# Folding the per-head maps into k's and q's weights: 64-by-64 tiles of three heads, four side by side, in place of 120 rows by 128 columns, with x's first transposes put ahead of the first modulation sums

## The chip, the cores and the metric

The kernel runs on one core of a Trainium2 chip. The metric is the device time of one execution in microseconds; lower is better. The core has TensorE (PE in the profile, its weight loads PEld), VectorE (DVE), ScalarE (ACT), GpSimd (POOL) and SyncE (SP, which here issues DMA transfers). TensorE writes to PSUM banks, the other compute engines read them. Everything is computed in float32, or in pairs of a rounded "high" part and the rest, the "low" part.

## The reference: what is computed

One transformer block for 2048 tokens of width 640 with 32 heads of 20. A condition vector `c` gives six rows of modulation (shift, scale and gate for each half). Attention is linear: each head's q and k go through a 20-by-20 matrix `w_phi[h]` and a softmax of both signs. A two-layer network with squared ReLU follows.

```
mod = (_silu(c) @ w_mod)                      # sa, ca, ga, sb, cb, gb
h = _layernorm(x) * (1 + ca) + sa
q, k, v = split(h @ wqkv)                     # 32 heads of 20
pq = einsum("bhsd,hdf->bhsf", q, w_phi);  pk = the same of k
phi = concat(softmax(p), softmax(-p))
o = phi_q @ (phi_k^T v) / (phi_q @ sum(phi_k))
x = x + ga * (o @ wo)
h = _layernorm(x) * (1 + cb) + sb
x = x + gb * (relu(h @ w1 + b1)**2 @ w2 + b2)
```

Since `pq` is linear in h, the kernel multiplies q's and k's weights by the heads' matrices once (the fold), and projects h with the folded weights. The change is in this fold.

## The kernel before, in words

**Stages.** The first 34 us load and prepare the weights of k and q, normalise the first 256 tokens and compute the modulation. Then a loop over 16 tiles of 128 tokens projects k, v and q and sums phi_k^T v; a second loop makes the attention's output; a third does the two-layer network. Up to the first projections of q and v, the order of the instructions on all five engines is the order in which the code is written (`manual_schedule`), so the order of the lines 625 to 662 is the order on each engine.

**Loads (lines 208 to 246).** SP issues, in this order: five chunks of k's weights (`load_raw`, lines 213 to 220), x's first 256 tokens, four chunks of q's weights, two chunks `wm` of modulation weights, q's fifth chunk, three more `wm`, x's second 256 tokens, five chunks of v's weights. A chunk of k's or q's weights is 320 KB, one of `wm` and one of x 640 KB. The host has transposed and reordered the weights of k and q: chunk d holds in 120 of 128 rows the features of six heads in each of five groups, and beside them the 128 input features of chunk d as columns. The 40 features of the last two heads lie in an array of their own (100 KB), loaded behind the first chunk.

**Block-diagonal matrix `bd_t` (lines 157 to 162, 248 to 258).** GpSimd makes a mask `own`, which says which of 120 rows belong to which of six heads. VectorE multiplies it with the heads' matrices (`bdc`, loaded by ScalarE's queue) in three operations.

**The fold (`fold`, lines 272 to 292).** For k and for q, and for each of five chunks of 128 input features, TensorE takes the raw weights as the stationary operand, 120 rows by 128 columns, and `bd_t` as the moving one, 120 columns for each of five groups of six heads and 40 for the last. The result, 128 input features by 640, fills two PSUM banks: the first three groups (360 columns) in the first, the rest (280) in the second. Banks come from a pool of four (`pj`, two folds' worth); only the fold of q's chunk 0 uses two banks of `kvp`. In the profile these matmuls are `foldk`, `foldq` and `kvp` of line 282. Each float32 matmul shows as two pairs of LDWEIGHTS and MATMUL, so a fold is 12 pairs.

`split` (lines 287 to 290) then takes each bank: ScalarE copies it to the rounded high part (line 289), VectorE subtracts that from the bank for the low part (the helper `lo`, line 90).

**The order around it (lines 623 to 662).** TensorE warms up with nine matmuls of ones (line 625) while the data come, and does five folds of k and four of q. In between VectorE takes the statistics of x (`stats`, lines 560 and 561, with a few operations on GpSimd, lines 562 to 565), and ScalarE scales x by them (`scale`, line 570). Then come, for chunk 0 of the modulation, `mod_rows2` (line 586: ten small matmuls of 32 columns that spread over four column tiles), `mod_sb` (line 594: ScalarE copies the sums from PSUM, `msb`), the ten transposes of x (`t_in`, line 364), `mod_cols2` (line 599: TensorE transposes `msb`; line 601: VectorE reduces it to shift and scale, `cols_a`), and `out0` (lines 375, 376 and 90: ScalarE applies shift and scale to x and rounds, `hfa` and `hT`; VectorE makes the low part). Chunk 1 of the modulation, q's fifth fold, chunk 2 and then the first projection of k (`k_step`, line 80, `pk`) follow. The split of q's fold 3 is written behind the transposes.

Of the kernel before, what the change touches and what calls it, by code (L numbers as in the profile page):

```python
# [53 lines left out]
def kernel(  # L54
# [19 lines left out]
    nc = tc.nc  # L74
# [14 lines left out]
    def lo(out_lo, full, hi, eng=None):  # L89
        (eng or nc.vector).tensor_tensor(out_lo, full, hi.bitcast(F32), op=ALU.subtract)  # L90
# [4 lines left out]
    def over(ap):  # L95
        return ap[:, :, None].to_broadcast([ap.shape[0], ap.shape[1], DH])
# [28 lines left out]
    def wslot(name, tag="w", pool=None):  # L125
        return tok2(tag, name, W2_AT if name.startswith("w2_") else 0, pool).bitcast(F32R)
# [26 lines left out]
    nc.gpsimd.memset(ones, 1.0)  # L153

    bdc = row("s3", "bdc")
    own = bdc[:120, P : P + 6]
    nc.gpsimd.memset(own, 1.0)
    nc.gpsimd.affine_select(out=own, in_=own, compare_op=ALU.is_ge, fill=0.0, base=0,
                            pattern=[[-DH, 6]], channel_multiplier=1)
    nc.gpsimd.affine_select(out=own, in_=own, compare_op=ALU.is_ge, fill=0.0, base=DH - 1,  # L160
                            pattern=[[DH, 6]], channel_multiplier=-1)
# [43 lines left out]
    nc.gpsimd.tensor_tensor(mask5, mask5, mtmp[:80, :40], op=ALU.add)  # L205


    nc.scalar.dma_start(bdc[:120, :120], bd)
# [12 lines left out]

    def load_x(j):
        XB[j] = tok2(f"x{j % 2}", f"xb{j}")
# [6 lines left out]
    def flat(e):  # L230
        return e.rearrange("p s d -> p (s d)")

    load_raw("k", wk5, wk1)
    load_x(0)
    load_raw("q", wq5, wq1, range(4))
    for d in range(2):
        load_wm(d)
# [7 lines left out]
        RV[d] = both[:, d % 2]  # L245
        nc.sync.dma_start(RV[d], wv[d * P : (d + 1) * P])

    by_head = bdc[:120, :120].rearrange("p (g f) -> p g f", f=DH)
    for a, b in ((0, 3), (3, 5)):
        nc.vector.tensor_tensor(  # L250
            bd_t[:120, 120 * a : 120 * b].rearrange("p (g i f) -> p g i f", i=6, f=DH),
            by_head[:, a:b, None, :].to_broadcast([120, b - a, 6, DH]),
            own[:, None, :, None].to_broadcast([120, b - a, 6, DH]), op=ALU.mult
        )
    nc.vector.tensor_tensor(
        bd_t[:120, 600:].rearrange("p (i f) -> p i f", f=DH),
        by_head[:, 5:6, :].to_broadcast([120, 2, DH]), over(own[:, :2]), op=ALU.mult
    )

    cs = const.tile([P, NC], F32, name="cs")  # L260
# [11 lines left out]
    def fold(nm, d, p=None):  # L272

        w = wslot(f"w{nm}{d}")
        W[nm, d] = w
        p = p or pj(f"fold{nm}{d}")
        for g, (o, n) in enumerate(GR):
            if g < 5:
                r = raw[nm][d // 2][:120, d % 2, g * P : (g + 1) * P]
            else:  # L280
                r = raw[nm][2][:120, 1, d * P : (d + 1) * P]
            nc.tensor.matmul(  # L282
                p[g // 3][:, (g % 3) * 120 : (g % 3) * 120 + n], r, bd_t[:120, g * 120 : g * 120 + n],
                start=True, stop=True,
            )

        def split():
            for h, (a, b) in enumerate(((0, 360), (360, 640))):
                nc.scalar.activation(w[:, 0, a:b], p[h][:, : b - a], AF.Copy)
                lo(w[:, 1, a:b], p[h][:, : b - a], w[:, 0, a:b])  # L290

        return split

# [64 lines left out]
    def by_turn(ap):  # L358
        return ap.rearrange("p (f b) -> p b f", b=NC)

    def t_in(xn, d, p, mixed=False):
        for i in range(2):
            src = by_turn(xn[:, i])[:, d] if mixed else xn[:, i, d * P : (d + 1) * P]
            nc.tensor.transpose(p[:, i * P : (i + 1) * P], src, ident)  # L364
# [207 lines left out]
    def half(b, h):  # L572
        return kvp[b][:, 256 * h : 256 * h + 256]
# [3 lines left out]
    def mod_rows2(*ds):  # L577

        p = tp(f"mrow{ds[0]}")
        for m, d in enumerate(ds):  # L580
            MR[d] = p[:, m * P : m * P + P]
            for k in range(NC):
                for s in range(2):
                    c = 2 * (k % 2) + s
                    a = 256 * k + P * s
                    nc.tensor.matmul(  # L586
                        MR[d][32 * c : 32 * c + 32], cs[:, k : k + 1].to_broadcast([P, 32]), WM[d][:, a : a + P],
                        start=(k < 2 and m == 0), stop=(k >= NC - 2), skip_group_check=True,
                    )

    def mod_sb(*ds):
        for d in ds:
            t = MR[d, "sb"] = row("s1", f"msb{d}")[:, :P]
            nc.scalar.activation(t, MR[d], AF.Identity, bias=plus[:, 0:1])
# [11 lines left out]
    TR = [half(0, 0), half(1, 0), half(1, 1), half(2, 0), half(2, 1)]  # L606
# [19 lines left out]
    for d in range(4):  # L626
        fold("k", d)()
# [16 lines left out]
    split = fold("q", 4)  # L644
# [68 lines left out]
    for t in range(2, NT - 2):  # L713
        j, i = divmod(t, 2)
# [12 lines left out]
        p = proj("v", t, *([(1, 0, lambda: t1(j + 1, 4))] if t == NT - 3 else []))  # L727
# [492 lines left out]
    for j in range(NB):  # L1220
        nxt = j + 1 < NB
        b, c = 2 * j + 5, 2 * j + 6
# [63 lines left out]
        if j == 7:  # L1286
            t2(0, 4)
            p = tp("gbt")[:NC, :P]
# [512 lines left out]
```

## Time and profile before

| | us |
|---|---|
| median of 3 runs (lowest to highest) | 751.52 (750.88 to 751.8) |
| the profiled execution's own time | 751.83 |
| its span, first to last instruction | 750.1 |
| what lies around the span | 1.7 |
| TensorE busy | 744.9 (99%) |
| VectorE, ScalarE, GpSimd busy | 601.4, 457.5, 169.0 |

| stretch, us | TensorE busy | weight loads | VectorE | ScalarE | DMA share, GB/s |
|---|---|---|---|---|---|
| 5.05 to 12.40 (k's folds) | 7.35 | 7.35 | 4.76 | 3.89 | 1.02, 377 |
| 12.40 to 17.86 (q's folds 0 to 3) | 5.46 | 5.41 | 4.06 | 4.13 | 1.04, 410 |
| 17.86 to 23.14 (modulation, fold 4) | 5.28 | 4.40 | 2.94 | 3.56 | 1.02, 408 |
| 23.14 to 34.00 (k's first projection) | 10.86 | 10.49 | 4.88 | 7.71 | 1.04, 388 |

A busy TensorE says little by itself: matmuls overlap, and the length of one (275 ns for one of the fold's) is several times the distance at which they follow each other. The distance is what counts, and it is read from a count of matmuls and the time that they take together. The names on the left of an arrow are written, those on the right read; numbers such as `128x360` are partitions by elements.

### The profile page before, as it was taken

What the parts mean: (1) busy time and instruction counts of PE and PEld (TensorE: products, weight loads), DVE (VectorE), ACT (ScalarE), POOL (GpSimd) and SP (SyncE); (2) the same over time, 40 slices, a digit from 0 to 9 for tenths busy, and PEclk for the clock granted to TensorE, in tenths of its full rate; (3) what the DMA queues carried; (4) which work ended last, traced back from release to release, by engine and by line L of the source; (5) the groups of instructions that cost most, each with busy time, mean ns of one, the idle gap of its engine ahead of it and who ended that gap; (6) DMA issues with size and microseconds to landing.
All of it is one profiled execution on the core that took longest, in us unless ns stands there. A gap on an engine that the chain in (4) does not pass through costs nothing.

```text
span 750.1 us, 15320 instructions
## 1 busy us (share of the span) xinstructions
PE 744.9 (99%) x5854; PEld 728.3 (97%) x5854; DVE 601.4 (80%) x1089; ACT 457.5 (61%) x1065; POOL 169.0 (23%) x355
## 2 busy tenths in 40 slices
PE   9999999999999999999999999999999999999998
PEld 9999999999999998998999999999999999999997
DVE  6598987988998899999665778777777776777766
ACT  5767666667863355557587766475574756647431
POOL 3000101000100237647303040132221313223110
PEclk9999999999999999999999999999999999999999
DMA  9811432343432254663885576797667767667461
GB/s 330 335 36 77 155 93 81 107 140 107 137 101 81 57 189 160 150 148 109 195 236 183 158 212 227 252 343 204 180 198 200 222 183 227 191 172 218 127 184 36
DMA packets 58796, 126.39 MB, mean 168 GB/s; under 512 B 7438, under 2 KB 16403, under 8 KB 58723
## 3 DMA queue, kind: packets, MB, share of 16 engines
q1 hardware_dynamic: 38636, 79.20, 32.2%
q0 software_dynamic: 17504, 40.90, 21.8%
q10 hardware_dynamic: 2583, 5.30, 1.9%
q8 instruction: 46, 0.75, 0.4%
q14 instruction: 27, 0.22, 0.1%
HBM read 100.74 MB, written 29.89 MB: 174 GB/s over the span
## 4 chain that ended last, share of the span: by engine, by line
PE 98%; ACT 1%; DVE 1%; POOL 0%; issue 0%; ACTq 0%; POOLq 0%
PE up L80 25%; PE acc L80 18%; PE pq L80 9%; PE pk L80 9%; PE pv L80 9%; PE pwo L80 9%; PE acc3x L80 5%; PE kvp L457 3%; PE te L954 2%; PE numa L80 1%; PE foldk L282 1%; PE numb L80 1%; PE ta L364 1%; PE foldq L282 1%; PE warm L625 1%; PE mrow L586 1%
## 5 line engine op out<-in xcount | busy, mean ns | idle before, releaser
L80 PE MATMUL up<-h,w 128*128 128x256 f32 x1640 | 204.6, 276 | 0.1
L80 PEld LDWEIGHTS up<-h,w 128*128 128x128 f32 x1640 | 196.5, 188 | 0.7 <-DVE h L90 0.5
L1350 ACT ACTIVATE ft<-up,b_t 128x256 f32<-128x256 f32 x104 | 49.0, 471 | 96.0 <-PE up L80 95.6
L80 PE MATMUL acc<-w,ra 128*128 128x384 f32 x452 | 97.5, 335 | 0.0
L80 PE MATMUL pwo<-wo,ot 128*128 128x384 f32 (+1 forms) x480 | 78.4, 314 | 0.0
L1351 DVE TENSOR_TENSOR ft<-ft 128x256 f32<-128x256 f32 x104 | 43.8, 421 | 43.1 <-ACT ft L1350 41.4
L80 PE MATMUL pq<-wq,hT 128*128 128x384 f32 (+1 forms) x480 | 75.6, 312 | 0.0
L80 PEld LDWEIGHTS acc<-w,ra 128*128 128x128 f32 x452 | 72.7, 188 | 0.8 <-DVE ra L90 0.6
L80 PE MATMUL pk<-wk,hT 128*128 128x384 f32 (+1 forms) x480 | 72.7, 308 | 0.0
L80 PEld LDWEIGHTS pwo<-wo,ot 128*128 128x128 f32 x480 | 69.7, 188 | 2.8 <-issue 2.7
L80 PEld LDWEIGHTS pq<-wq,hT 128*128 128x128 f32 x480 | 71.1, 188 | 0.6 <-issue 0.2
L80 PE MATMUL pv<-wv,hT 128*128 128x384 f32 (+1 forms) x480 | 71.6, 306 | 0.0
L80 PEld LDWEIGHTS pk<-wk,hT 128*128 128x128 f32 x480 | 70.5, 188 | 0.4 <-issue 0.2
L80 PEld LDWEIGHTS pv<-wv,hT 128*128 128x128 f32 x480 | 70.0, 188 | 0.0
L90 DVE TENSOR_TENSOR ra<-ft,ra 128x384 fp32r<-128x384 f32 (+2 forms) x86 | 36.8, 449 | 32.6 <-ACT ra L1374 20.0
L1460 POOL DMA_DIRECT2D ring_a<-td_a x34 | 18.5, 543 | 116.9 <-PE acc L80 103.6
L1374 ACT ACTIVATE ra<-ft 128x384 fp32r<-128x384 f32 x48 | 25.2, 526 | 28.4 <-DVE ft L1351 22.4
L80 PE MATMUL acc3x<-w,ra 128*128 128x256 f32 x231 | 39.5, 278 | 0.0
L80 PEld LDWEIGHTS acc3x<-w,ra 128*128 128x128 f32 x231 | 37.2, 188 | 0.0
L1365 DVE TENSOR_TENSOR ft<-ft 128x128 f32<-128x128 f32 x136 | 33.3, 286 | 1.2
L448 DVE TENSOR_REDUCE sk<-ek 128x64 f32<-128x1280 f32 x16 | 23.7, 1484 | 12.8 <-ACT ek L443 10.8
L341 POOL TENSOR_SCALAR sma<-sma 128x2 f32<-128x2 f32 x6 | 1.8, 298 | 137.2 <-ACT xb L340 137.2
(270 smaller groups left out, 1470.2 us busy)
## 6 DMA issues: line engine op xcount, KB each, us to landing
ring_c<-td_c POOLq DMA_DIRECT2D x34, 384.0 KB, 3.8
ring_a<-td_a POOLq DMA_DIRECT2D x34, 384.0 KB, 3.4
ring_b<-td_b POOLq DMA_DIRECT2D x34, 256.0 KB, 3.6
esp<-eq SPq DMA_DIRECT2D x12, 640.0 KB
el<-esp SPq DMA_DIRECT2D x12, 640.0 KB
rw<-in_w SPq DMA_DIRECT2D x23, 320.0 KB
wm<-in_w_mod SPq DMA_DIRECT2D x20, 320.0 KB
xb<-in_x SPq DMA_DIRECT2D x8, 640.0 KB
```

The lines of the kernel that those rows point to most:

```text
L80: nc.tensor.matmul(o, a, b, start=first and i == 0, stop=last and i == len(terms) - 1, skip_group_check=skip,)
L90: (eng or nc.vector).tensor_tensor(out_lo, full, hi.bitcast(F32), op=ALU.subtract)
L282: nc.tensor.matmul(p[g // 3][:, (g % 3) * 120 : (g % 3) * 120 + n], r, bd_t[:120, g * 120 : g * 120 + n], start=True, stop=True,)
L364: nc.tensor.transpose(p[:, i * P : (i + 1) * P], src, ident)
L448: nc.vector.tensor_reduce(s, heads(flat(e)), axis=AX.X, op=ALU.add)
L457: nc.tensor.matmul(kvp[g // 4][64 * c : 64 * c + 64, a : a + 2 * n].rearrange("p (s n) -> p s n", s=2), v[:, u], e[:, :, o : o + n], start ...
L954: nc.tensor.transpose(p[:124, a : a + P], EU[2 * j + i][:, 2 * g + c, :124], ident)
L1350: nc.scalar.activation(r, p, AF.Relu, bias=b1_t[:, f : f + 1])
L1351: nc.vector.tensor_tensor(r, r, r, op=ALU.mult)
L1365: nc.vector.tensor_tensor(t[:, o], t[:, a], t[:, b], op=op)
L1374: nc.scalar.activation(a[:, 0, :3], t[:, :3], AF.Copy)
L1460: nc.gpsimd.dma_start(RING[j, n, r], TD[n][r].bitcast(F32R))
```

## The change

The fold is cut otherwise. The 32 heads are split in two halves of 16, one on rows 0 to 59 of each chunk and one on rows 64 to 123 (rows 60 to 63 and 124 to 127 are zero); a group is three heads (60 rows) of each half, and there are five groups and one of one head. For each group four matmuls of 64 rows by 64 columns with 60 moving columns (20 in the last group) go to the four quarters of the array: rows 0 and 64, columns 0 and 64. The half by rows selects the PSUM bank, the half by columns its partitions. So a fold has 24 matmuls, 48 pairs, for 6 matmuls and 12 pairs; both banks hold 320 columns and are written until the fold's end. The host lays out the raw weights and the heads' matrices to match, with as many bytes in all for the weights; the last heads' rows come in two transfers of 20 rows. `bd_t` needs one multiply of 360 columns, and the mask one more operation on GpSimd.

In the order, the ten transposes of x come ahead of the first `mod_rows2`, and the split of q's fold 3 directly behind its fold, ahead of `mod_sb`.

```diff
+FOLDS = [(60 * g, 60) for g in range(5)] + [(300, DH)]
...
-                nc.sync.dma_start(raw[nm][2][:40, 1], w1)
+                for a in range(2):
+                    nc.sync.dma_start(raw[nm][2][64 * a : 64 * a + DH, 1], w1[DH * a : DH * a + DH])
...
-        for g, (o, n) in enumerate(GR):
-            if g < 5:
-                r = raw[nm][d // 2][:120, d % 2, g * P : (g + 1) * P]
-            else:
-                r = raw[nm][2][:120, 1, d * P : (d + 1) * P]
-            nc.tensor.matmul(
-                p[g // 3][:, (g % 3) * 120 : (g % 3) * 120 + n], r, bd_t[:120, g * 120 : g * 120 + n],
-                start=True, stop=True,
-            )
+        for g, (o, n) in enumerate(FOLDS):
+            r = raw[nm][d // 2][:, d % 2, g * P : (g + 1) * P] if g < 5 else raw[nm][2][:, 1, d * P : (d + 1) * P]
+            for a in (0, 64):
+                for c in (0, 64):
+                    nc.tensor.matmul(
+                        p[a // 64][c : c + 64, o : o + n], r[a : a + 64, c : c + 64], bd_t[a : a + 64, o : o + n],
+                        start=(g == 0), stop=True, skip_group_check=True,
+                    )
 
         def split():
-            for h, (a, b) in enumerate(((0, 360), (360, 640))):
-                nc.scalar.activation(w[:, 0, a:b], p[h][:, : b - a], AF.Copy)
-                lo(w[:, 1, a:b], p[h][:, : b - a], w[:, 0, a:b])
+            for h, (a, b) in enumerate(((0, HALF), (HALF, D))):
+                nc.scalar.activation(w[:, 0, a:b], p[h][:, :HALF], AF.Copy)
+                lo(w[:, 1, a:b], p[h][:, :HALF], w[:, 0, a:b])
...
-    split = fold("q", 3)
+    fold("q", 3)()
+    for d in range(NC):
+        t_in(XB[0], d, TR[d])
     mod_rows2(0)
     mod_sb(0)
-    for d in range(NC):
-        t_in(XB[0], d, TR[d])
-    split()
     mod_cols2(0)
```

On TensorE, around q's fold 3 and the first modulation sums, before (`foldq` is the fold, `mrow` the sums, `kvp<-ident,xb` the transposes of x, `kvp<-ident,msb` that of the copied sums):

```order
L282 MATMUL foldq_0_357<-bd_t,raw_q_146 128x120 x3
L282 MATMUL foldq_1_358<-bd_t,raw_q_146 128x120 x2
L282 MATMUL foldq_1_358<-bd_t,raw_q_147 128x40
L586 MATMUL mrow_365<-wm_154,cs 32x128 x10
L364 MATMUL kvp_76<-ident,xb_143 128x128 x2
L364 MATMUL kvp_77<-ident,xb_143 128x128 x4
L364 MATMUL kvp_78<-ident,xb_143 128x128 x4
L599 MATMUL kvp_76<-ident,msb_376 128x128
L586 MATMUL mrow_398<-wm_156,cs 32x128 x10
```

The same place with the change, from the last full group of the fold on:

```order
L280 MATMUL foldq_0_502<-bd_t,raw_q_148 64x60 x2
L280 MATMUL foldq_1_503<-bd_t,raw_q_148 64x60 x2
L280 MATMUL foldq_0_502<-bd_t,raw_q_149 64x20 x2
L280 MATMUL foldq_1_503<-bd_t,raw_q_149 64x20 x2
L362 MATMUL kvp_76<-ident,xb_145 128x128 x2
L362 MATMUL kvp_77<-ident,xb_145 128x128 x4
L362 MATMUL kvp_78<-ident,xb_145 128x128 x4
L584 MATMUL mrow_542<-wm_157,cs 32x128 x10
L597 MATMUL kvp_76<-ident,msb_553 128x128
L584 MATMUL mrow_561<-wm_159,cs 32x128 x10
```

The transposes have moved from between the sums and the transposition of `msb` to the front of the sums; the two banks of a fold (`foldq_0`, `foldq_1`) now take turns instead of one after the other.

On ScalarE at the same place, before (`wq<-foldq` are a fold's two copies, `xb` the scaling of x, `hfa` and `hT` the first use of shift and scale):

```order
L570 ACTIVATE xb_143<-xb_143,nba_293,sqa_292 128x640 x2
L289 ACTIVATE wq_343<-foldq_0_344 128x360
L289 ACTIVATE wq_343<-foldq_1_345 128x280
L594 ACTIVATE msb_376<-mrow_365,plus 128x128
L289 ACTIVATE wq_356<-foldq_0_357 128x360
L289 ACTIVATE wq_356<-foldq_1_358 128x280
L375 ACTIVATE hfa_0_394<-kvp_76,cols_a 128x256
```

And with the change:

```order
L568 ACTIVATE xb_145<-xb_145,nba_366,sqa_365 128x640 x2
L287 ACTIVATE wq_470<-foldq_0_471 128x320
L287 ACTIVATE wq_470<-foldq_1_472 128x320
L287 ACTIVATE wq_501<-foldq_0_502 128x320
L287 ACTIVATE wq_501<-foldq_1_503 128x320
L592 ACTIVATE msb_553<-mrow_542,plus 128x128
L373 ACTIVATE hfa_0_557<-kvp_76,cols_a 128x256
```

The copies of q's fold 3 have passed the copy of the first sums. VectorE's order is the same but for the one multiply in place of three; behind this place all engines do what they did, in the same order.

More of the change, by code (lines that the diff above doesn't have):

```diff
@@ L155 @@
     bdc = row("s3", "bdc")
[L156 to L161, printed above, removed]
+    own6 = bdc[:, 120:126]
+    own = own6[:, :3]
+    nc.gpsimd.memset(own6, 1.0)
+    o6 = own6.rearrange("p (a i) -> p a i", a=2)
+    nc.gpsimd.affine_select(out=o6, in_=o6, compare_op=ALU.is_ge, fill=0.0, base=0,
+                            pattern=[[-64, 2], [-DH, 3]], channel_multiplier=1)
+    nc.gpsimd.affine_select(out=o6, in_=o6, compare_op=ALU.is_ge, fill=0.0, base=DH - 1,
+                            pattern=[[64, 2], [DH, 3]], channel_multiplier=-1)
+    nc.gpsimd.tensor_tensor(own, own, own6[:, 3:], op=ALU.add)
     ident = const.tile([P, P], F32, name="ident")
@@ L246 @@
         nc.sync.dma_start(RV[d], wv[d * P : (d + 1) * P])
[L248 to L253, printed above, removed]
-        )
     nc.vector.tensor_tensor(
-        bd_t[:120, 600:].rearrange("p (i f) -> p i f", f=DH),
-        by_head[:, 5:6, :].to_broadcast([120, 2, DH]), over(own[:, :2]), op=ALU.mult
+        bd_t[:, :360].rearrange("p (g i f) -> p g i f", i=3, f=DH),
+        bdc[:, :120].rearrange("p (g f) -> p g f", f=DH)[:, :, None, :].to_broadcast([P, 6, 3, DH]),
+        own[:, None, :, None].to_broadcast([P, 6, 3, DH]), op=ALU.mult
     )
@@ L1762, in by_chunk @@
     def by_chunk(w):
-        t = np.zeros((P, 5, D), w.dtype)
-        t[:120] = w.T[:600].reshape(5, 120, D).transpose(1, 0, 2)
-        return t.reshape(P, 5, NC, P).transpose(2, 0, 1, 3).reshape(NC * P, D), w.T[600:]
+        w = w.T.reshape(2, HALF, D)
+        t = np.zeros((2, 64, 5, D), w.dtype)
+        t[:, :60] = w[:, :300].reshape(2, 5, 60, D).transpose(0, 2, 1, 3)
+        return t.reshape(P, 5, NC, P).transpose(2, 0, 1, 3).reshape(NC * P, D), w[:, 300:].reshape(2 * DH, D)
     wq5, wq1 = by_chunk(A_wqkv[:, :D])
@@ L1779 @@
         "wv": A_wqkv[:, 2 * D :][:, VCOLS],
-        "bd": bd.reshape(120, 120),
+        "bd": bd.reshape(P, 120),
         "c": c.reshape(NC, P).T,
```

8 lines of the change are left out of this document (4 added, 4 removed).

## Prediction

> **What bounds the kernel now.** First the page: who carries the chain that ended last, and at which clock.
>
> ```profile
> PE 98%; ACT 1%; DVE 1%; POOL 0%; issue 0%; ACTq 0%; POOLq 0%
> PEclk9999999999999999999999999999999999999999
> ```
>
> TensorE sets the end nearly everywhere, at full clock. So a microsecond taken off TensorE early in the program is a microsecond off the end, if TensorE does not wait for anything later. The waits of TensorE from 33 us to the end, and the largest of its weight loads', are these:
>
> ```profile
> PE tail L936 <- POOL rn L1160: 0.4, 1, 0.4
> PEld pwo L80 <- issue: 2.7, 7, 0.4
> ```
>
> No engine or transfer makes it wait there for more than a few tenths; what follows the change is carried along. Then the chain in order of time over the first 30 us (start, length, what):
>
> ```profile
> 1.05 4.21 PE warm L625 x18
> 5.26 7.31 PE foldk L282 x60
> 12.57 1.34 PE kvp L282 x12
> 13.91 4.02 PE foldq L282 x36
> 17.93 0.78 PE mrow L586 x20
> 18.71 1.24 PE kvp L364 x10
> 19.95 0.11 PE kvp L599
> 20.06 0.78 PE mrow L586 x20
> 20.84 1.46 PE foldq L282 x12
> 22.30 0.14 PE kvp L599
> 22.44 0.78 PE mrow L586 x20
> ```
>
> The ten folds are TensorE back to back: nine from 5.26 to 17.93, the tenth at 20.84. One fold is 12 pairs of weight load and matmul (six float32 matmuls, two passes each): 4.02 us / 36 = 111.7 ns a pair, 1.34 us a fold. Ten folds are 14 us; this is all that the change can shorten.
>
> What stands behind TensorE in this stretch is seen in the rows of ScalarE and VectorE: the copy of a fold's result (two halves), the subtraction for its low part, and the statistics of x.
>
> ```profile
> 6.56 0.47 ACT L289 ACTIVATE wk<-foldk 128x360 fp32r<-128x360 f32 x1 [1.77 <-PE foldk L282]
> 7.99 1.01 ACT L289 ACTIVATE wk<-foldk 128x360 fp32r<-128x360 f32 x2 [0.33 <-PE foldk L282]
> 17.60 0.74 ACT L289 ACTIVATE wq<-foldq 128x360 fp32r<-128x360 f32 x2
> 7.06 1.07 DVE L90 TENSOR_TENSOR wk<-foldk,wk 128x360 fp32r<-128x360 f32 x2 [1.36 <-ACT wk L289]
> 14.85 0.88 DVE L90 TENSOR_TENSOR wq<-kvp,wq 128x360 fp32r<-128x360 f32 x2
> 15.65 0.88 DVE L90 TENSOR_TENSOR wq<-foldq,wq 128x360 fp32r<-128x360 f32 x2
> 12.07 0.88 DVE L560 BATCH_NORM_STATS2 sta<-xb 128x6 f32<-128x320 f32 x2
> 15.96 1.73 ACT L570 ACTIVATE xb<-xb,nba,sqa 128x640 f32<-128x640 f32 x2 [0.27 <-POOL nba L565]
> ```
>
> Unhindered, a fold's two subtractions take 0.80 us of VectorE (14.85 to 15.65) and its two copies 0.7 us of ScalarE (17.60). Both are under 1.34, but not by so much that a fold of 0.7 us would be followed at its own pace.
>
> **What the folds become.** A fold is now 24 matmuls of 64 rows by 64 columns with 60 moving columns, 48 pairs, for four tiles of the array. Whether tiles run side by side is read from other code. The modulation sums put four tiles of 32 columns beside one another; the rows count their matmuls that run in each short window (window, length, busy and count):
>
> ```profile
> 19.98:20.02 0.04, 0.03 (x4) 1.00 0.63 256
> 20.02:20.12 0.10, 0.10 (x4) 1.00 1.26 512
> 20.12:20.16 0.04, 0.04 (x8) 1.00 0.31 128
> ```
>
> Four start within 0.04 us, none in the next 0.10, then four more: waves of four. Two tiles that differ in their rows (the sums z, 64 rows each) also start together, in two banks:
>
> ```profile
> 252.50:252.54 0.04, 0.02 (x2) 1.00 0.00 0
> 252.54:253.02 0.48, 0.48 (x2) 1.00 0.00 0
> ```
>
> And tiles with 64 columns of weights, two side by side, 120 moving columns:
>
> ```profile
> 60.85 2.54 PE L457 MATMUL kvp<-ek,vt 128*64 128x120 f32 x44
> 60.84 2.38 PEld L457 LDWEIGHTS kvp<-ek,vt 128*64 128x64 f32 x44
> ```
>
> 44 pairs in 2.38 us are 54 ns a pair, 108 ns for a wave of two. So tiles cut by columns and tiles cut by rows each run in parallel, weight loads included. No row shows both cuts at once; I take it that four run. A wave then has half the columns of a full pair on either side (64 for 128 to load, 60 for 120 to stream): 111.7 / 2 = 56, and I take 58 ns. Twelve waves: 0.70 us a fold. The bounds: nothing in the trace issues pairs for long closer than the modulation sums do,
>
> ```profile
> 25.19 1.50 PE L586 MATMUL mrow<-wm,cs 128*32 128x128 f32 x40
> ```
>
> (1.50 - 0.27) / 40 = 31 ns (0.27 being one matmul's own length, below), or 1.49 us a fold; and 56 ns a wave is the least.
>
> The Trainium skill, TensorE: Matmul & The Clock Gate, section Back-to-back issue gap, speaks against this change: starts of matmuls never come closer than about 25 ns however few columns they have. By that, a fold of 48 pairs takes 1.20 us, an estimate from that page. The windows above disagree for different tiles (four starts within 0.04 us), but only in bursts.
>
> **What follows a fold.** A fold's halves used to be ready one after the other (first half after six pairs, so its copy ran under the second); now all four tiles end together. A bank pair is used by every second fold, and its next fold waits for both subtractions. The cycle of a pair: fold 0.70, end of matmul to copy 0.25 (kvp's 0.27, less for fewer columns), first copy 0.44 (0.47 for 360 columns, now 320) and handover 0.03, two subtractions 0.88, handover 0.04: 2.34 us for two folds, 1.17 a fold instead of 1.34. So half of the saving of TensorE is lost to this cycle.
>
> In detail, in the clock of the trace. Fold k0 starts at 5.05 (the warming matmuls end, 0.1 for the other tile shape); the array is still slow there (warm: 4.21 us / 18 = 234 ns for a pair that later takes 112), so it takes 1.4 us; copies from 6.74, subtractions from 7.2 (7.06 before): no gain. k1's subtractions follow at 8.0; k2's fold waits for k0's subtractions, 8.1 to 8.8, subtractions 9.5; k3's 10.3 to 11.1. The statistics of x thus start at 11.1 for 12.07: **1.0 us early**. Scaling x follows 3.89 later, as before (15.96 - 12.07): 15.0, ending 16.7. ScalarE is free for it: the last copies ahead are q1's, whose data end at 3.15 MB, just behind the 3.03 of the last row quoted below, so that they are through by 14.4.
>
> VectorE, after the statistics (2.0 us: the row at 14.85 is the second subtraction of a fold's after them), does k4, q0, q1 at 0.80 each: until 15.5. Fold q3 needs q1's banks: 15.6 to 16.3. Then the moved transposes: the first at 16.5 (0.2 for the change of tile shape, as in the next rows), the second when x's second half is scaled, 16.7, the last nine at 0.11 each (10 in 1.07): 17.7. The first modulation sum then starts at 17.9, where it starts now (17.86); but the transposes lie behind it.
>
> ```profile
> 17.86 0.85 PE L586 MATMUL mrow<-wm,cs 128*32 128x128 f32 x20
> 18.64 1.07 PEld L364 LDWEIGHTS kvp<-ident,xb 128*128 128x128 f32 x10 [0.20 <-issue]
> 19.79 0.27 PE L599 MATMUL kvp<-ident,msb 128*128 128x128 f32 x1
> 18.76 0.37 ACT L594 ACTIVATE msb<-mrow,plus 128x128 f32<-128x128 f32 x1 [0.42 <-PE mrow L586]
> 21.11 0.42 ACT L376 ACTIVATE hT<-hfa 128x256 fp32r<-128x256 f32 x1
> 21.43 0.35 ACT L594 ACTIVATE msb<-mrow,plus 128x128 f32<-128x128 f32 x1
> 22.37 0.85 PE L586 MATMUL mrow<-wm,cs 128*32 128x128 f32 x20
> ```
>
> This is also where the move costs: the transposes used to cover the copy of the sums (msb, 18.76 to 19.13). That cover is gone: the first sums end at 18.75, msb at 19.15, and TensorE stands idle for about half a microsecond before the transposition of msb (L599), which comes at 19.2 for 19.79. Behind it wait the second sums: 19.46 for 19.99, **0.5 us early**. Done alone, with the old folds, the move would cost this 0.5. q2's and q3's copies, which now both stand between the scaling and msb on ScalarE, take 0.7 each and end at 18.0, before the sums do: nothing.
>
> Fold q4 takes 0.70 for 1.34 and another 0.2 for its shape. Then the second L599 waits for msb, which stands on ScalarE behind the chain from the first L599 (hT, msb): 21.1 for 22.13. The third sums: 21.38 for 22.37, **1.0 us early**. (The same steps with the durations of before put them at 22.5, 0.14 late; against that, 1.12. I take 1.1.) All that follows waits for these sums or for matmuls behind them, and is carried along.
>
> Edits that cost nothing: the mask of heads has one more operation on GpSimd, on 128 by 3 numbers, and one VectorE multiply replaces three; the warming matmuls cover both, and without that cover each would cost its tenths of a microsecond once. Each last-heads load is two DMAs for one: 0.4 us more of SP's issue, twice. What stands behind them, the data, runs ahead of use: by 11.0 us the queue has moved
>
> ```profile
> q1 hardware_dynamic: 1319, 3.03, 79.1%
> ```
>
> 3.03 MB, past k, x's first tiles (they end at 2.40 MB) and q's first chunk (2.72 MB). At no more than the 512 GB/s of the windows above, x's last bytes came 1.2 us earlier or more, at 9.8; with a delay of 0.4 they are still ahead of the 11.1 at which VectorE is free.
>
> **Sum.** -1.1 us: the profiled execution's 751.83 becomes 750.7, and the median of the runs shown, 751.52 (0.3 below it), becomes **750.4**. Some 0.2%, 1.5 us, is what a measurement of this kernel can tell from no change; the forecast lies inside.
>
> **Rivals.** *Slower: pairs are not issued fast enough.* If 480 pairs in a row come no faster than the sums' 31 ns, a fold takes 1.49 us, later than today's, and without the early first half: the cycle is 3.13 for two folds. By the same steps the statistics start at 13.2, the scaling at 17.1, q3's fold ends at 19.3, and the third sums stand at 25.0 for 22.5: +2.5, 754.0. For it: no longer row is closer. Against: those waves are as long as their 128 moving columns need, so the row need not be a limit of issue. The point of decision is about 1.0 us a fold (21 ns a pair): there the loss at the bank cycle and the move eat the gain. The Trainium skill's 25 ns (same page and section) would give 752.6.
>
> *Slower too: tiles run two by two, not four*, so that the change doesn't do what it says: 24 waves of 58 ns, 1.39 us a fold, by the same steps +2.0, 753.5. For it: only one cut at a time is seen. Against: in the sums four tiles already take four different streams from the same rows, so that four at a time are not new.
>
> *Faster: the bank cycle binds less.* If the next fold starts on the first bank while the second is still read, the subtractions follow each other at 0.80: k3's end at 10.4, x is there, the statistics start 1.6 early, and later gains add: about -1.7, 749.8. For it: tiles on the first bank need only that bank. Against: TensorE takes its instructions in order, and the second bank's stand between.
>
> *Nearly nothing*: a wave of 70 to 90 ns, -0.7 to +0.5.
>
> **How the numbers follow.** Forecast (-0.4 to -1.5) 0.57; faster rival 0.20; nearly nothing 0.07; issue 0.09; two by two 0.07. Faster by over 0.2% (under 750.0): the faster rival and the edge of the forecast, 0.22; slower by over 0.2% (over 753.0): issue and two by two, 0.16; within, 0.62. The range leaves out these two slower cases and takes in the page's 25 ns and 56 ns waves with the faster rival: 749.5 to 752.8.
>
> **What would show it.** Right: folds of 64x60 with about 0.7 us each and gaps between them, in which TensorE waits for VectorE's subtraction or for data; VectorE's statistics near 11.1; scaling near 15.0; a hole of 0.5 us before the first L599; third sums near 21.4. Wrong: folds over 1.0 us, statistics after 12; or statistics before 10.7 and third sums before 21.0; or a clock below full in the stretch, since TensorE is idle for a third of it; or a gain at 21.4 that is gone by the end.

## The result, and the profile after

The changed kernel takes **759.83 us** (median of 4 runs, 759.69 to 760.02), the kernel before 751.2 (750.78 to 751.8) beside it: ratio 1.0111, 95% interval 1.0098 to 1.0124. Forecast was 750.4, with a range of 749.5 to 752.8. The profiled execution spans 758.0 us, that of before 750.1.

The page of the changed kernel: the chain that ended last by engine, the granted clock, and a queue of instructions (packets, MB, share), which the counts below show to be TensorE's.

```profile
PE 94%; DMA 2%; issue 1%; ACT 1%; DVE 1%; POOL 0%; SPq 0%; ACTq 0%; POOLq 0%
PEclk9999999999999999999999999999999999999999
q8 instruction: 49, 0.80, 0.5%
```

"Issue" is at 1% of 758 us, where it was 0%: some 7 us in which an engine waited for nothing that the profile shows. The 2% of DMA are transfers that the chain passes through; TensorE waits for one only twice, 0.2 us at the start and 0.4 us later. The last line looks harmless and is where the answer lies. Over 40 slices the clock seems full; a slice is 19 us, and what happened is shorter. The chain in order of time (start, length, what), from k4's fold to k's projection:

```profile
10.41 0.33 PE foldk L280 x7
10.74 3.47 issue
14.21 1.12 PE foldk L280 x31
...
17.69 2.70 issue
...
25.10 0.57 PE mrow L584 x15
25.66 0.98 issue
26.65 0.44 PE mrow L584 x5
...
28.64 0.82 PE foldq L280 x48
...
29.75 0.78 PE mrow L584 x20
...
36.52 5.18 PE pk L81 x36
```

TensorE stops three times, for 3.47, 2.70 and 0.98 us, each time in the middle of something: in k4's fold, in a fold of q, between the 15th and 16th pair of one set of sums. There no matmul needs anything that the one ahead of it did not need. The stops sum up to 7.15 us, and the third sums (29.75) are 7.31 later than before (22.44); k's last projection part starts 7.7 later (28.83 before), the span is 7.9 longer. So nearly all of the loss is made by 30 us and carried along.

Where a stop falls is told by counting. TensorE's rows of the timeline between the first two stops (start, length, instruction, count, idle time before it):

```profile
14.21 1.12 PE L280 MATMUL foldk<-bd_t,raw_k 64*64 64x60 f32 x33 [3.47 <-issue]
15.10 0.34 PE L280 MATMUL kvp<-bd_t,raw_q 64*64 64x60 f32 x2
15.11 0.36 PE L280 MATMUL foldk<-bd_t,raw_k 64*64 64x20 f32 x4
15.23 1.37 PE L280 MATMUL kvp<-bd_t,raw_q 64*64 64x60 f32 x42
16.38 0.34 PE L280 MATMUL foldq<-bd_t,raw_q 64*64 64x60 f32 x2
16.39 0.36 PE L280 MATMUL kvp<-bd_t,raw_q 64*64 64x20 f32 x4
16.51 1.18 PE L280 MATMUL foldq<-bd_t,raw_q 64*64 64x60 f32 x41
20.39 3.15 PE L280 MATMUL foldq<-bd_t,raw_q 64*64 64x20 f32 x101 [2.70 <-issue]
```

33 + 2 + 4 + 42 + 2 + 4 + 41 = 128 matmuls; with 127 weight loads and one semaphore instruction of TensorE they are 256 instructions from stop to stop. Counted in this way from the start of the program, the three stops lie behind 449, 705 and 961 instructions. And the page's 6214 matmuls and 6214 loads, over 49 packets of that queue, are 254 a packet. **A packet is a block of 256 instructions, and TensorE stops where a block ends and the next has not come.** From the end of one stop to the end of the next it is 6.18 us (14.21 to 20.39), then 6.26 (26.65). One block per 6.2 us is 48 ns a pair; a fold of 48 pairs in 0.82 us wants them at 17.

Before, the 120 pairs that the chain in the prediction counts from 13.91 to 23.22 take 9.3 us, so that 128 take 9.9 and the next block is always there.

The clock did fall (window, length, busy time and count of TensorE, its weight loads, VectorE, ScalarE and GpSimd, then the clock, DMA share, GB/s):

```profile
10.70:14.20 3.50, 0.04 (x3) 0.00 (x0) 2.89 (x8) 0.25 (x1) 0.16 (x1) 0.96 1.06 355
14.20:17.60 3.40, 3.39 (x128) 3.35 (x127) 1.33 (x4) 1.53 (x4) 1.23 (x4) 0.54 1.01 402
...
20.40:25.40 5.00, 5.00 (x126) 4.68 (x127) 2.57 (x6) 3.69 (x8) 0.00 (x0) 0.66 1.02 402
```

0.54 behind the first stop, 0.66 on average over the 5 us behind the second. And in the first stop, as behind it, the DMA engines are full (shares of 1.0 and more).

### The profile page after: what moved, and what is told of

Its sections match the earlier page's. It is cut to its first block, busy times and chain, and to the rows that moved or that the text cites. A ratio compares the mean times of both kernels' runs of the same rounds, so it can differ in the third digit from the quotient of the medians.

```text
span 758.0 us, 16040 instructions
## 1 busy us (share of the span) xinstructions
PE 744.2 (98%) x6214; PEld 725.5 (96%) x6214; DVE 601.2 (79%) x1087; ACT 456.8 (60%) x1065; POOL 169.0 (22%) x356
## 4 chain that ended last, share of the span: by engine, by line
PE 94%; DMA 2%; issue 1%; ACT 1%; DVE 1%; POOL 0%; SPq 0%; ACTq 0%; POOLq 0%
PE up L81 24%; PE acc L81 17%; PE pq L81 9%; PE pk L81 9%; PE pv L81 9%; PE pwo L81 8%; PE acc3x L81 5%; PE kvp L455 3%; PE te L951 2%; PE numa L81 1%; PE numb L81 1%; PE ta L362 1%; PE foldq L280 1%; DMA ring_a<-td_a 1%; DMA td_a<-tst_a 1%
## 5 line engine op out<-in xcount | busy, mean ns | idle before, releaser
L81 PE MATMUL acc3x<-w,ra 128*128 128x256 f32 x231 | 39.5, 277 | 0.0
```

What stands on the lines that cost most here:

```text
L81: nc.tensor.matmul(o, a, b, start=first and i == 0, stop=last and i == len(terms) - 1, skip_group_check=skip,)
```

## The experiments

**The theory.** Instruction supply: blocks of 256 come through the same DMA engines as the data, one per 6.2 us here; 960 instructions of folds use them up faster. **Rivals:** a wait for data or a buffer that the profile does not show; the tiles or the clock (TensorE idles between short folds); the move of the transposes.

### Transposes back in their old place

```diff
-    fold("q", 3)()
-    for d in range(NC):
-        t_in(XB[0], d, TR[d])
-    mod_rows2(0)
-    mod_sb(0)
+    split = fold("q", 3)
+    mod_rows2(0)
+    mod_sb(0)
+    for d in range(NC):
+        t_in(XB[0], d, TR[d])
+    split()
```

> The tiled folds as changed, with x's transposes back behind the first modulation sums and q3's copies behind those. Theory (instruction supply): TensorE's instructions come in blocks of 256 and the folds now use them up faster than blocks arrive; the count of instructions up to any place is nearly the same, so TensorE stops again in the middle of a fold for about 3.5 us near 10.7, 2.7 us near 17.7 and 1 us near 25.5, and the time is 759.3 (758.8 to 760.2). Rival (the move of the transposes is the cost): the stops go, 750 to 752.

758.75 us, ratio 1.0092 (1.0079 to 1.0106), just under the lower end expected. TensorE's timeline:

```profile
13.61 0.83 PE L280 MATMUL foldk<-bd_t,raw_k 64*64 64x60 f32 x34 [2.87 <-issue]
...
19.79 1.02 PE L280 MATMUL foldq<-bd_t,raw_q 64*64 64x20 f32 x53 [2.82 <-issue]
...
25.96 1.23 PE L362 MATMUL kvp<-ident,xb 128*128 128x128 f32 x5 [0.33 <-issue]
```

The stops stay, 6.18 and 6.17 us from one to the next. The third now cuts x's transposes in two, where the change has the sums: the same count (449, 705 and 961 again), other work. The move is not the cause.

### Two tiles of 64 by 128 in place of four of 64 by 64

```diff
             for a in (0, 64):
-                for c in (0, 64):
-                    nc.tensor.matmul(
-                        p[a // 64][c : c + 64, o : o + n], r[a : a + 64, c : c + 64], bd_t[a : a + 64, o : o + n],
+                nc.tensor.matmul(
+                    p[a // 64][:, o : o + n], r[a : a + 64], bd_t[a : a + 64, o : o + n],
```

> Each fold with two tiles of 64 rows by 128 columns in place of four of 64 by 64: 24 pairs, 48 instructions, where the change has 96; layout, copies and order stay as changed. Theory (instruction supply): 256 instructions are 5.3 folds, which at the 1.17 us of the bank cycle are 6.2 us, as long as a block took to come in the changed kernel; the stops are gone or sum up to under 1 us, the clock stays full, and the time is 750 to 753, according to whether a wave of two takes 56 or 112 ns. Rival (tiles of 64 rows, or a TensorE that idles between short folds, lose the clock): half clock between 10 and 20 us and 755 or more. Rival (a wait for data that the profile does not show): stops of 3 us at the same folds, 757 or more.

763.94 us (six runs, 758.79 to 767.92), ratio 1.0157 (1.0127 to 1.0187): slower than all that was expected, and for another reason. TensorE's timeline:

```profile
5.19 12.99 PE L279 MATMUL foldk<-bd_t,raw_k 64*128 64x60 f32 x120
```

In the profiled execution there is no stop and the clock is full, but 12.99 / 120 = 108 ns a pair, 2.6 us a fold. The two tiles do start together, but the next two only 213 ns later, twice as long as a pair of the whole array (112). The bounds of 56 to 112 ns were wrong; what holds the next two back is not shown. At this pace a block lasts 13 us, so that the run tells nothing for or against the supply; against the clock it tells nothing either, since TensorE never idles.

### More instructions ahead of the folds

```diff
-    for i in range(WARM):
+    for i in range(WARM - 4):
         nc.tensor.matmul(warm[:, :P], ones, ones, start=True, stop=True)
+    for i in range(34):
+        nc.tensor.matmul(warm[:64, :4], ones[:64, :64], ones[:64, :4], start=True, stop=True)
```

> The changed kernel with the last four of nine warming matmuls (16 instructions) replaced by 34 tiny ones (136), which take about as long; all else as changed. Theory (instruction supply): the stops stand at fixed counts from the program's start, 256 apart, so the first comes 120 instructions earlier: no longer 13 pairs into k4's fold at 10.7 us but about 37 pairs into k1's, at 7.5 to 8, and lasts until about 12; time 760.5 (759.5 to 762). Rival (a wait for data or a buffer that the profile does not show): the first stop stays in k4's fold near 10.7, about as long, 759.8.

765.2 us (one run). The tiny pairs, all in one tile, took 107 ns each (68 in 7.3 us); so the folds began only at 10.6, and the times expected are void. The place was also miscounted: 120 instructions ahead of the first stop lies the start of k3's fold, not a place in k1's. There TensorE did wait until 16.63, behind 449 instructions as in the changed kernel, but also for VectorE, so that this stop by itself proves nothing. What holds is the count of the next ones. The timeline:

```profile
16.63 2.77 PE L280 MATMUL foldk<-bd_t,raw_k 64*64 64x60 f32 x96 [1.49 <-DVE wk L91]
19.21 1.10 PE L280 MATMUL kvp<-bd_t,raw_q 64*64 64x60 f32 x31
22.81 0.63 PE L280 MATMUL kvp<-bd_t,raw_q 64*64 64x60 f32 x17 [2.50 <-issue]
23.26 3.43 PE L280 MATMUL foldq<-bd_t,raw_q 64*64 64x60 f32 x110
29.04 0.76 PE L280 MATMUL foldq<-bd_t,raw_q 64*64 64x60 f32 x34 [2.35 <-issue]
```

96 + 31 and 17 + 110 matmuls, with their weight loads (128 and 126) and semaphore instructions (one and three) 256 instructions each time, in 6.18 and 6.23 us. The stops that cut a later fold of q and the sums now cut q0's fold (`kvp`) and another one: they keep their count and lose their place in the work. A wait for data or buffers would have kept the place.

### A run of tiny pairs, DMA engines idle and busy

These two kernels measure the supply by itself: behind k's projection of the kernel before, 640 pairs on four tiles of 128 rows by 32 columns. The second kernel adds a copy in memory alongside (the first two added lines).

```diff
+    if d == NC - 1:
+        nc.sync.dma_start(dram.tile([D, 6 * D], F32, name="copy"), w_mod)
+    burst = tp("burst")
+    for i in range(320):
+        c = 32 * (i % 4)
+        nc.tensor.matmul(burst[c : c + 32, :4], ones[:, :32], ones[:, :4], start=True, stop=True,
+                         skip_group_check=True)
```

> The kernel before, with 640 pairs (1280 instructions) of tiny matmuls, 128 rows by 32 columns and four moving columns, put in behind the k projection of the first tokens (near 34 us), where the DMA engines soon carry nothing. Adds work that the output does not use. Theory (instruction supply): TensorE stops within the run of tiny matmuls, 256 instructions apart, with nothing to wait for; a block takes about 4.1 us there (1.75 from the switch of blocks to the packet, 0.95 for it, 1.4 to the next start, from rows of the changed kernel), so the time grows by 14 to 18 us. Rival (pairs are limited in their issue, not in their supply): even spacing without stops, at one rate throughout.

> The kernel before with the same 640 tiny pairs at the same place as in the run with idle DMA engines, and beside them one copy of the w_mod matrix (9.8 MB) from memory to memory, which keeps the DMA engines busy through that run of pairs. Adds work that the output does not use; later loads wait behind the copy, so the total time says nothing and only the stretch is read. Theory (instruction supply, in competition with the data): the stops stand at the same counts (961, 1217, 1473, 1729), but a block takes about 6.2 us, as in the changed kernel, and not 3.45. Rival (load of the DMA engines does not matter; the 6.2 us are due to something else in the folds): 3.45 us again.

769.07 us the first (+17.3 on the kernel before, 14 to 18 expected; one run), 787.15 the second (one run; its later loads wait behind the copy). TensorE's timeline, idle DMA engines:

```profile
33.48 1.50 PE L667 MATMUL burst<-ones 128*32 128x4 f32 x158
37.22 1.25 PE L667 MATMUL burst<-ones 128*32 128x4 f32 x128 [2.25 <-issue]
40.67 1.89 PE L667 MATMUL burst<-ones 128*32 128x4 f32 x128 [2.20 <-issue]
44.13 1.89 PE L667 MATMUL burst<-ones 128*32 128x4 f32 x128 [1.57 <-issue]
```

Busy DMA engines:

```profile
34.19 1.75 PE L669 MATMUL burst<-ones 128*32 128x4 f32 x158
40.94 1.89 PE L669 MATMUL burst<-ones 128*32 128x4 f32 x128 [5.00 <-issue]
49.61 1.89 PE L669 MATMUL burst<-ones 128*32 128x4 f32 x128 [6.78 <-issue]
58.27 1.89 PE L669 MATMUL burst<-ones 128*32 128x4 f32 x128 [6.77 <-issue]
```

These are the plainest lines here: the same instructions at the same place, 128 pairs between stops both times, and a block takes 3.45 us (37.22 to 40.67) with idle and 8.67 (40.94 to 49.61) with busy engines; 6.2 was expected there. This copy moves in packets of 60 KB, the loads in 2.5 to 5 KB; that this makes the difference is not shown. The blocks behind these two take 3.46 and 4.00 us, and 8.66 and 6.74. The 128 pairs themselves take 1.25 us, and 1.89 in the rows where the clock is halved (0.50). The idle engines show what the 3.45 are made of (DMA engines by window: slices of busy share, then the packets):

```profile
DMA  0900000000000000000000000000000000000000
q8 instruction: 1, 0.02, 5.6%
```

This is the window from 38.3 to 39.5. TensorE goes over to a new block at 37.22; in the records of the transfers one packet then runs from 38.35 to 39.42, the only one, and at 40.67 TensorE goes on. So 1.1 us pass ahead of the packet, 1.1 in it, 1.25 behind it. In the changed kernel TensorE goes over at 14.21, the packet runs from 17.80 to 18.82, TensorE goes on at 20.39: packet and what follows are nearly as long, and 3.6 us pass ahead of it, beside data. That is where the load of the DMA engines enters. The Trainium skill, Runtime: NRT & Kernel Launch, section Instruction fetch mechanics, says the same of the blocks (256 instructions, the next fetched by DMA while one is executed), but holds the fetch to be hidden, as instructions are issued more slowly than they come. By that rule there would be no stops; in these two runs and in the changed kernel the trace disagrees, with 13.5 ns an instruction at best (3.45 us / 256) and 24 beside the loads.

### Less data beside the folds

The changed kernel with zeros in place of the loads of the modulation's and v's weights:

```diff
-        nc.sync.dma_start(WM[d], w_ss[d * P : (d + 1) * P])
+        nc.gpsimd.memset(WM[d], 0.0)
...
-        nc.sync.dma_start(RV[d], wv[d * P : (d + 1) * P])
...
+    for d in range(NC):
+        nc.gpsimd.memset(RV[d], 0.0)
     v_hi(0)
```

> The changed kernel, but the five loads of the modulation weights (640 KB each) and the five of v's weights are replaced by zeros written on GpSimd, so that the DMA engines have little to carry from 13 us on; instructions of TensorE and their order are the changed kernel's. Leaves out the modulation and v. Theory (instruction supply, in competition with the data): the first stop stays, 2.5 to 3.5 us; from then on a block takes the 3.45 us of the run of tiny matmuls instead of 6.2, so the second stop shrinks from 2.7 to 0.8 us or less and the third is gone; 755.5 to 757.5. Rival (a block takes 6 us whatever the DMA engines carry at the time): stops of 2.7 and 1 us as before, 759 to 760.

758.17 us (one run), between what the theory and the rival gave. The third stop is gone, as expected. The second is not: 15.13 to 19.36, even longer than the 2.70. The windows:

```profile
13.30:15.20 1.90, 1.90 (x128) 1.90 (x127) 1.12 (x4) 1.17 (x4) 1.16 (x3) 1.00 1.04 395
15.30:19.30 4.00, 0.05 (x3) 0.00 (x0) 0.89 (x3) 0.20 (x1) 0.20 (x1) 0.90 0.65 231
19.40:22.60 3.20, 3.20 (x102) 3.11 (x103) 1.06 (x3) 2.91 (x7) 0.00 (x0) 0.50 0.02 5
```

The expectation had overlooked the loads that remain: 395 GB/s until x's second tiles are in, near 18. The packet for this block began only at 17.01. The next, asked for at 19.36 with nothing left to carry, began 1.24 us later, and there the stop is missing. A second reading: here 128 pairs ran at full clock in 1.9 us and the stop lasted 4.2; in the changed kernel they ran at half clock in 3.4 and the stop lasted 2.7. Both make 6.1 to 6.2. With more instructions ahead of the folds the clock stayed full between the second and the third stop (1.00), and that block took 6.23. **While blocks are late, the halved clock costs nothing; it only shortens the stop.**

### Old folds, transposes moved

```diff
-    split = fold("q", 3)
-    mod_rows2(0)
-    mod_sb(0)
+    fold("q", 3)()
     for d in range(NC):
         t_in(XB[0], d, TR[d])
-    split()
+    mod_rows2(0)
+    mod_sb(0)
```

> The kernel before with the transposes of x and q3's copies moved ahead of the first modulation sums, and nothing else. The prediction's step: the move alone costs 0.5 us, the half microsecond in which TensorE waits for the copy of the sums that the transposes used to cover; the ratio to before is 1.0005 to 1.001. With these folds a block of 256 instructions lasts 10 us, so TensorE makes no stop without a reason in the profile. Rival (the move costs what the two orders of the tiled kernel differ by): +1.1 us, ratio 1.0015.

752.53 us, ratio 1.0009 (1.0001 to 1.0018), +0.1 to +1.4 us. That takes in the rival's 1.0015 too. No stop without a reason; the idle time is where it was foretold, and as long:

```profile
19.93 0.33 PE L599 MATMUL kvp<-ident,msb 128*128 128x128 f32 x1 [0.47 <-ACT msb L594]
```

### New rows alone

No fold tiled, old order, weights in the new rows; one matmul of 128 rows and 128 columns writes both halves.

```diff
+            nc.tensor.matmul(
+                p[g // 3][:, : 2 * y].rearrange("p (a x) -> p a x", a=2)[:, :, 60 * (g % 3) : 60 * (g % 3) + n],
+                r, bd_t[:, 120 * g : 120 * g + 2 * n].rearrange("p (a x) -> p a x", a=2), start=True, stop=True)
```

> The kernel before with the weights in the new rows (60 of 64 partitions, last heads by two transfers, mask and copies to suit), no fold tiled and the old order. Theory: only the data come later, by the 0.2 to 0.4 MB that the changed kernel is behind at 14 us: +0.3 to +1.0 us, ratio 1.0004 to 1.0013, no stop, full clock. Rival (rows and copies cost more, and explain a good part of the 8 us): 1.003 or more.

752.37 us, ratio 1.0008 (0.9999 to 1.0017): as expected in size, though no more than "same" can be claimed. Its timeline shows what has no counterpart before:

```profile
12.76 1.53 PE L295 MATMUL kvp<-bd_t,raw_q 128*128 128x120 f32 x12 [0.97 <-DMA raw_q<-in_wq]
```

q0's fold waits for its data. By 14 us the queue of the loads had carried 3.77 MB here, 4.18 in the kernel before, and 4.01 and 4.02 in two others in the old rows (the moved transposes and the idle run of pairs).

### A few folds tiled

The same kernel with some folds in four tiles: k0 to k2; q3 and q4; and, with the last heads on 40 adjoining partitions so that one transfer brings them, q3 and q4 and then q2 to q4.

```diff
+TILED = ("q3", "q4")
...
+            if tiled:
+                for a in (0, 64):
+                    for c in (0, 64):
...
-                for a in range(2):
-                    nc.sync.dma_start(raw[nm][2][64 * a : 64 * a + DH, 1], w1[DH * a : DH * a + DH])
+                nc.sync.dma_start(raw[nm][2][64 - DH : 64 + DH, 1], w1)
```

> As the kernel with the last two folds tiled, but with k0, k1 and k2 tiled instead and q3 and q4 not: the same tiles at the same places as in the changed kernel, up to 9 us. Theory (instruction supply): the 449 instructions that are there at the start reach to q1's fold near 14.5, when the next block, asked for near 7.4, has come (14.2); no stop or one under 0.5 us, full clock, time 751 to 752 for 751.8 before (the folds that follow gain only the bank cycle's 0.17 us each). Rival (TensorE idles between short folds, so that the clock is halved): half clock near 14 us also here, 754 or more.

> The order of before and the weights in the new rows, but only the folds q3 and q4 in four tiles; the other eight are one tile of 128 rows by 128 columns with 120 moving columns (12 pairs), whose output columns are put in the order of heads. Theory (instruction supply): 432 instructions of folds for 960, a block of 256 lasts longer than the 6.2 us in which one comes, so there are no stops and the clock stays full; q3 and q4 take 0.7 to 0.8 us for 1.34, and as neither waits for banks, the time is 1.0 us less than before (0.6 to 1.3), ratio 0.9985. Rival (tiled folds cost the stops or the clock whatever their number): slower than before by 2 us or more.

> As the kernel with the last two folds tiled, but the rows of the last heads lie on 40 partitions next to each other (44 to 83), so that one transfer brings them as before, not two. Theory: in the kernel with the last two folds tiled the gain went into the data: two more transfers hold back every later one (the sums' third load landed at 22.8), so with one transfer each the loads run as before and the time falls by the 1.0 us that was expected there: 750.8 for 751.8, ratio 0.9975 to 0.9992. Rival (the gain of tiled q3 and q4 is lost on TensorE, not on data): 0.9997 as there.

> The same with q2's fold tiled as well: 504 instructions of folds. Theory (instruction supply): still no stop, since 256 instructions last longer than 6.2 us; q2 is followed by q3's wait for its banks, so it brings less than q3 and q4: another 0 to 0.5 us; ratio 0.9970 to 0.9992. Rival (one more tiled fold brings the stops back): a stop near instruction 449 or 705 and a time above that of before.

| tiled | us | ratio (95%) | stops |
|---|---|---|---|
| k0 to k2 | 752.91 | 1.0020 (1.0010 to 1.0030) | none |
| q3, q4 | 751.5 | 0.9997 (0.9988 to 1.0006) | none |
| q3, q4, one transfer | 751.58 | 0.9997 (0.9987 to 1.0006) | none |
| q2 to q4, one transfer | 753.43 | 1.0028 (1.0015 to 1.0040) | one |

With k0 to k2 tiled TensorE runs the same tiles at the same places as the change up to 9 us, and at 10.7 it does not stop; it waits later, with a reason, and the clock stays full:

```profile
12.98 1.53 PE L295 MATMUL kvp<-bd_t,raw_q 128*128 128x120 f32 x12 [1.18 <-DMA raw_q<-in_wq]
```

So neither the tiles nor short folds with idle time between them bring the stops or the half clock. What the early tiles gained went into waiting for q0's data; the time came out 0.9 above the upper end expected.

The last row is the point of decision. With q2 tiled too, the chain has a stop in the middle of x's transposes:

```profile
19.48 0.87 issue
20.35 2.02 PE kvp L380 x9
```

TensorE's timeline has the whole of it:

```profile
20.35 2.02 PE L380 MATMUL kvp<-ident,xb 128*128 128x128 f32 x9 [1.69 <-ACT wq L305]
```

The releaser named there, and the part of the stop ahead of 19.48 that the chain gives to ScalarE, are not the reason: with q3 and q4 alone the same transposes run from 18.34 on, while ScalarE makes these copies (18.72 to 19.48). This stop, too, lies behind 449 instructions.

One more tiled fold is 72 instructions more. The block that had to come was asked for at 14.20 at the latest, came at 20.34 (6.14 us), and was needed behind the matmul at 18.33. With q3 and q4 alone it was needed at 21.5 and 20.6 and nobody waited. "No stop" was expected, so the budget had been set too loosely; the rule it was set by holds. With q3 and q4 tiled, these folds took 0.8 to 1.0 us for 1.34, but the gain of 1.0 was not measured in either kernel. In the first, the second and third sums waited for their weights; the second:

```profile
20.57 0.85 PE L606 MATMUL mrow<-wm,cs 128*32 128x128 f32 x20 [0.38 <-DMA wm<-in_w_ss]
```

In the second these waits are gone (third sums at 21.76 in its profiled execution), but its times are the same: 0.9997, as the rival had it, where 0.9992 at most was expected. Where the gain is lost stays open. One transfer for two did not bring the data back either: 3.71 MB by 14 us. Why data in the new rows are 0.1 to 0.5 MB behind stays open too. No version here is measurably faster than the kernel before.

## Why the prediction was wrong, point by point

- **The step that failed** stands in "What the folds become": "Twelve waves: 0.70 us a fold", with the bound that "nothing in the trace issues pairs for long closer than the modulation sums do", 31 ns a pair. It prices 480 pairs by how TensorE takes them, and their supply at nothing. Supplied are 128 pairs per 6.2 us, 48 ns a pair, shown by the counts, the two runs of tiny pairs and the fold too many. Beside the stops nothing of the forecast gain is left: the third sums are 7.31 us later for 7.15 us of stops, where 1.1 earlier was forecast. Once blocks set the pace, what TensorE saves only makes the stops longer. The queue's row stood on the page of before too, and the working does not use it:

```profile
q8 instruction: 46, 0.75, 0.4%
```

- **The fold's own length was right.** Where nothing is missing, 48 pairs take 0.82 us with the change of shape (28.64 in the chain; forecast 0.70 and 0.2), and its waves of four start 58 ns apart (eight steps from 28.73 to 29.20; 58 was forecast). Four tiles do run side by side, 17 ns a pair, so that the rival "two by two" falls. The Trainium skill's 25 ns between starts (TensorE: Matmul & The Clock Gate, section Back-to-back issue gap) does not agree with that, nor with the tiny pairs on four tiles, which came at under 10 (128 in 1.25 us). "So tiles cut by columns and tiles cut by rows each run in parallel, weight loads included" holds less far: tiles cut by rows alone start together, but a wave of two takes 213 ns.
- **The bank cycle was right**: the loads of k3 and k4 start 1.10 apart, each behind VectorE's subtraction; 1.17 was forecast, and 0.80 by the rival "the bank cycle binds less".

```profile
9.30 0.90 PEld L280 LDWEIGHTS foldk<-bd_t,raw_k 64*64 64x64 f32 x48 [0.20 <-DVE wk L91]
10.40 0.21 PEld L280 LDWEIGHTS foldk<-bd_t,raw_k 64*64 64x64 f32 x8 [0.20 <-DVE wk L91]
```

- **Statistics of x at 11.1**: they came at 11.82. Of the 0.7 us, 0.4 are VectorE's, which ended k3's subtractions at 11.54 and not at 11.1; then it waited 0.28 for x. The step "with a delay of 0.4 they are still ahead of the 11.1" failed: a smaller error of the same kind, since the new rows were priced by SP's issue alone and not by what the data do.

```profile
11.82 0.89 DVE L558 BATCH_NORM_STATS2 sta<-xb 128x6 f32<-128x320 f32 x2 [0.28 <-DMA xb<-in_x]
```

- **The move at 0.5 us**: right (0.7, 0.1 to 1.4, and 0.47 us of waiting in the trace). With the tiled folds it and the old order differ by 0.0019 in ratio, 1.4 us, but those intervals overlap.
- **The rival "pairs are not issued fast enough"** named the right engine and sign, with 0.09, and put its price at 2.5 us, as it took 31 ns for the worst. The runs split the ratio of 1.0111 into 0.0008 for the rows alone, 0.0084 for the tiles in the old order (1.0092) and 0.0019 for the move among them: 0.6, 6.3 and 1.4 us, each uncertain by about 1 us.
- **Signs.** "A clock below full, since TensorE is idle for a third of it" was seen, but as a consequence: behind the stops, and at no cost of its own while blocks are late.

## What to carry to other kernels

Before one instruction of TensorE is cut into four, ask what feeds it: find the stretch's 256-instruction blocks (128 pairs), and compare the time TensorE needs for one with the time in which one comes, here 3.45 us with idle DMA engines and 6 to 9 with busy ones. Small tiles can pay only where a block lasts longer than that, which means a few folds among longer matmuls, not ten in a row during the loads; here even a few brought no gain that could be measured. A stop in the middle of a set of matmuls, "issue" without a releaser, at a multiple of 128 pairs, is this; a wait in the same place of the work is not.

## What the runs showed of the hardware, unexpected

- Instructions of TensorE share the DMA engines with data: the wait from a block's start to the packet for the next is 1.1 to 1.2 us with idle engines, 3.6 and 3.8 us in the second and third block of the changed kernel beside loads at 400 GB/s. By the same count of instructions it is 2.2 us in the kernel before (13.94 to 16.14) and 1.9 with two tiles (13.25 to 15.18), beside engines as full. TensorE does not wait for these blocks, and whether they were asked for ahead of the count or came sooner is not shown; the 6.2 us are measured where it waits.
- Two tiles of 64 rows by 128 columns take 213 ns a wave, four of 64 by 64 take 58, both with 60 moving columns and at full clock: the smaller tile is over three times faster at the same work.
- Tiny pairs (four moving columns, full clock) in one tile of 64 by 64 follow at 107 ns, on four tiles of 128 by 32 in turn at under 10.
